# Rearranging the MLP end of an adaLN decode kernel: features on partitions

## The chip, the cores and the metric

The kernel runs on one core of a Trainium2 chip. A core has TensorE (PE: matmuls, with a separate weight load, PEld), VectorE (DVE), ScalarE (ACT), GpSimd (POOL) and SyncE (SP), which here only issues transfers; 16 DMA engines carry them. SBUF is the on-chip memory of 128 partitions, PSUM the memory that matmuls write. The metric is device time in microseconds (us), the median of several runs.

## The reference

One decode step for four sequences (one new token each): adaLN modulation, attention over a cache of 4096 positions in 32 heads, then a gated MLP. The inputs are bfloat16.

```python
x = A_x                                          # (4, 1, 512)
mod = (_silu(c) @ w_mod).reshape(c.shape[0], 6, 1, -1)
sa, ca, ga, sb, cb, gb = (mod[:, i] for i in range(6))
h = _layernorm(x, axis=-1) * (1 + ca) + sa
x = x + ga * _A_ref(h, A_k_cache, A_v_cache, A_wq, A_wo)
h = _layernorm(x, axis=-1) * (1 + cb) + sb
x = x + gb * _B_ref(h, B_w_in, B_w_sp, B_b_sp, B_w_out)

def _B_ref(x, w_in, w_sp, b_sp, w_out):          # w_in 512 x 1792, w_out 896 x 512
    z = _gelu(jnp.einsum('bsd,df->bsf', x, w_in))
    z1 = z[..., :Fh].copy()
    z2 = _layernorm(z[..., Fh:], axis=-1)
    g = jnp.einsum('ts,bsf->btf', w_sp, z2) + b_sp[None, :, None]
    return jnp.einsum('bsf,fd->bsd', z1 * g, w_out)
```

`_A_ref` is ordinary attention: queries from `wq`, scores scaled by 128 ** -0.5, softmax, the sum over V, and the projection by `wo`. The sequence length is 1, so `w_sp` and `b_sp` are one number each. The K and V caches are 128 MB each and make up nearly all of the transfer.

## The kernel before

The order of instructions on each engine is the order of the program; nothing is moved by a scheduler. The attention runs over NT = 32 steps, each one pair of four heads (`HQ`) and one sequence, with a K tile and a V tile of 4 MB. SP issues all large loads in one queue: the modulation and query weights first, then K and V tiles, at step 2 `wo_sb` and `wo_last` (the projection weights of all groups but the last, and of the last), and in the last steps V in pieces (`TAIL`: 64, 32, 16 and 16 of 128 column blocks), then `win_sb` and `wout_sb` (L505, L507). A step multiplies K by the query on VectorE (L278), reduces it on TensorE (L284) and VectorE (L293), takes the softmax, and two steps later V is summed (`pv`, L353).

Step 2 also makes the modulation columns (`mod_cols`, L232: features on partitions, the four sequences as columns) and the gate rows `gps` (L477, copied to `gbr` at L482), which step 5 multiplies by the two numbers `w_sp` and `b_sp`.

The last step L is one of sequence `BL` = 3, the last row. Its V is summed by `o_last` (L389) in four parts that follow the pieces of `TAIL`, with V as the stationary operand. Between the parts, TensorE does the two products of the second layernorm for the rows known so far: `normed` (its `across` at L185 sums over partitions by a matrix of constants, its `summed` at L190 adds the blocks). Rows 0 to 2 are complete there; row 3 still lacks the last group of heads. That contribution, `last` (L540), is scaled and added after `o_scale` (L395) and `o_proj` (L405), and a second product (`st`, `mq2`) gives row 3's own mean and variance.

Then the MLP:

- L552: 56 matmuls, `win_sb` stationary, `hcs` moving. `hcs` has eight columns: the four rows as normed without their scale, and the four shifts `sb`. The scales `rs2` are made on ACT meanwhile (`rsqrt`, L194 and L195: Ln, then Exp) and are applied to the product by VectorE at L574; L575 adds the product of the shifts.
- L562 loads ACT's table for gelu, L577 and L581 take the gelu of the second half (`z2`, the gate) and of the first (`z1`), and L582 loads the table for Ln and Exp again.
- L583 and the `across` after it: sums of `z2` and of its square for the gate's layernorm.
- L593 (`w_out`): two passes of 28 matmuls each, with `z1w` (z1, in 32 columns, the unused ones zero) and `pw` (z1 * z2) as the stationary operand and `wout_sb` moving, 128 columns at a time; the four blocks of 128 output columns go to four column groups of TensorE. The outcome has rows on partitions.
- L604 to L617: the layernorm's mean and variance for each of these partitions, with a second Ln and Exp; L620 to L629: six operations on 128x128 tiles that put the two passes, the gate rows and the residual `x1r` (L568: the residual brought to the same layout by 16 small matmuls) together.
- L633: four transfers write the output.

Of the kernel before, what the change touches and what calls it, by code (L numbers as in the profile page):

```python
# [22 lines left out]
def kernel(  # L23
# [112 lines left out]
    st3 = consts.tile([P, 2, B, NH + 1], F32, name="st3")  # L136
    nc.vector.memset(st3, 0.0)
    nc.vector.memset(st3[:, 1, :, NH:], LN_EPS * FH / P)
# [7 lines left out]
    selb = consts.tile([P, B], F32, name="selb")  # L146
    idr = ident_f.rearrange("p (c g q) -> p g c q", g=R // HQ, q=HQ)
    for g in range(G):
        nc.vector.tensor_reduce(out=selg[:, g:g + 1], in_=idr[:, g], axis=AX.XY, op=ALU.add)
    nc.vector.tensor_reduce(  # L150
        out=selb, in_=ident_f.rearrange("p (c b) -> p b c", b=B), axis=AX.X, op=ALU.add
    )
    nc.vector.tensor_copy(out=sel4, in_=selb)
# [4 lines left out]
    z1w = consts.tile([P, NH, R], BF16, name="z1w")  # L158
    nc.gpsimd.memset(z1w, 0.0)
    pw = consts.tile([P, NH, R], BF16, name="pw")  # L160
    nc.gpsimd.memset(pw, 0.0)
    cTw = consts.tile([P, DJ, R], BF16, name="cTw")
    nc.gpsimd.memset(cTw, 0.0)
# [33 lines left out]
    def normed(pool, src, name, then=None):  # L197
# [11 lines left out]
        nc.vector.tensor_tensor(out=sq, in0=xb, in1=xb, op=ALU.mult)  # L209
        v = summed(pool, across(sq, inv_d), f"v_{name}")  # L210
# [14 lines left out]
    cT = cTw[:, :, 0:B]  # L225
    nc.vector.tensor_tensor(out=cT, in0=cx, in1=sg, op=ALU.mult)

    def mod_cols(s0, n, dst):
        for m in range(n):
            c0 = (s0 + m // DJ) * D + m % DJ  # L230
            for k in range(DJ):
                nc.tensor.matmul(  # L232
                    dst[:, m, :], lhsT=wm_sb[:, k, c0:c0 + (P - 1) * DJ + 1:DJ], rhs=cT[:, k, :],
                    start=(k == 0), stop=(k == DJ - 1),
                )
# [180 lines left out]
    hcs = consts.tile([P, DJ, 2 * B], BF16, name="hcs")  # L416
    gbr = consts.tile([P, P], F32, name="gbr")
    gbw = consts.tile([P, P], F32, name="gbw")
# [14 lines left out]
    for i in range(NT):  # L433
# [33 lines left out]
        if i == 2:  # L467
            nc.scalar.dma_start(out=sp_t[:, 0:1], in_=B_w_sp[0:1, 0:1])
            nc.scalar.dma_start(out=sp_t[:, 1:2], in_=B_b_sp.rearrange("(a b) -> a b", b=1))
            mps = ps_sm([P, 3 * DJ, B])  # L470
            mod_cols(2, 3 * DJ, mps)
            nc.vector.tensor_copy(out=modT, in_=mps)
            nc.vector.tensor_copy(out=hcs[:, :, B:2 * B], in_=mps[:, DJ:2 * DJ, :])
            gps = ps_sm([P, P])
            for k in range(DJ):
                for j in range(DJ):
                    nc.tensor.matmul(  # L477
                        gps[R * j:R * (j + 1), :], lhsT=cTw[:, k, :],
                        rhs=wm_sb[:, k, 5 * D + j * P:5 * D + (j + 1) * P],
                        start=(k == 0), stop=(k == DJ - 1), tile_position=(0, R * j),  # L480
                    )
            nc.vector.tensor_copy(out=gbr, in_=gps)  # L482
# [8 lines left out]
            nc.sync.dma_start(out=wo_last, in_=A_wo[hl:H * DH].rearrange("(q p) n -> p q n", p=P))  # L491
        if i == 5:
            sps = ps_sm([P, 2])
            nc.tensor.matmul(sps, lhsT=ones_b, rhs=sp_t, start=True, stop=True)
            nc.vector.tensor_copy(out=spf, in_=sps)
            for k, t in ((0, gbw), (1, gbr)):
                nc.vector.tensor_scalar(
                    out=t, in0=gbr, scalar1=spf[:, k:k + 1], scalar2=None, op0=ALU.mult
                )
            cbT = modT[:, 2 * DJ:3 * DJ, :]  # L500
            nc.vector.tensor_scalar_add(out=cbT, in0=cbT, scalar1=1.0)
# [7 lines left out]
    gaT = modT[:, 0:DJ, :]  # L509
    scores(L)  # L510
# [20 lines left out]
    xc, rs2 = normed(tl, x1, "ln2", lambda: o_last(L, 1))  # L531
    hc = hcs[:, :, 0:B]
    nc.vector.tensor_tensor(out=hc, in0=xc, in1=cbT, op=ALU.mult)

    o_last(L, 2)
    o_last(L, 3)
    o_scale(L)
# [6 lines left out]
    mq2 = summed(tl, across(st2, inv_d), "mq2")  # L544
    nc.vector.scalar_tensor_tensor(
        out=hc[:, :, BL], in0=xs, scalar=mq2[:, 0:1], in1=cbT[:, :, BL],
        op0=ALU.subtract, op1=ALU.mult,
    )
    zps = ps_q()[:, 0:NF * 2 * B].rearrange("p (f b) -> p f b", b=2 * B)
    for f in range(NF):  # L550
        for k in range(DJ):
            nc.tensor.matmul(  # L552
                zps[:, f, :], lhsT=win_sb[:, k, f * P:(f + 1) * P], rhs=hcs[:, k, :],
                start=(k == 0), stop=(k == DJ - 1),
            )
# [5 lines left out]
    rsqrt(rs2[:, BL:B], nv2, -1.0)  # L561
    nc.scalar.preload_act_table_set("gelu_apprx_tanh_and_others")  # L562
    nc.vector.tensor_tensor(out=x1[:, :, BL], in0=x1[:, :, BL], in1=last, op=ALU.add)
    x1r = ps_red()[:, 0:P]
    for k in range(DJ):
        for j in range(DJ):
# [4 lines left out]
            )  # L571

    z = tl.tile([P, NF, B], F32, name="z")
    nc.vector.tensor_tensor(out=z, in0=zps[:, :, 0:B], in1=bc(rs2, NF), op=ALU.mult)  # L574
    nc.vector.tensor_tensor(out=z, in0=z, in1=zps[:, :, B:2 * B], op=ALU.add)  # L575
    z2 = st3[:, 0, :, 0:NH]
    nc.scalar.activation(  # L577
        out=z2, in_=z[:, NH:, :].rearrange("p f b -> p b f"), func=AF.Gelu_apprx_tanh
    )
    z1 = tl.tile([P, NH, B], F32, name="z1")  # L580
    nc.scalar.activation(out=z1, in_=z[:, 0:NH, :], func=AF.Gelu_apprx_tanh)  # L581
    nc.scalar.preload_act_table_set("natural_log_exp_and_others")  # L582
    nc.vector.tensor_tensor(out=st3[:, 1, :, 0:NH], in0=z2, in1=z2, op=ALU.mult)  # L583
    ps3 = across(st3.rearrange("p g b f -> p g (b f)"), inv_f)
# [79 lines left out]
```

## Time and profile before

| what | us |
|---|---|
| median of 3 runs | 675.5 |
| the runs | 673.76, 675.5, 675.64 |
| the profiled execution, whole | 673.46 |
| its span, first to last instruction | 671.7 |
| TensorE busy | 405.1 (60%) |
| VectorE busy | 423.3 (63%) |
| ACT busy | 85.0 (13%) |
| GpSimd busy | 3.3 (0%), 15 instructions |
| DMA: bytes, mean rate | 283.19 MB, 422 GB/s |
| chain that ended last: DMA, VectorE, TensorE | 53%, 31%, 14% |
| last transfers issued, from SP and ACT | 668.90 |

The page cuts the span into 40 slices; a digit is the busy share in tenths.

```profile
PE   1185784466577655555666566666556457755766
DVE  3176593775666777566577666666776566777733
DMA  9999999999999999999999999999999999999994
```

The DMA engines are full in every slice but the last, which begins near 655 us. Times below are counted from the start of the span. In timeline lines, the columns are start and length in us, engine, source line, operation, what it writes from what, and in brackets how long its engine had been idle and what ended that.

### The profile page before, as it was taken

To read this page: it belongs to the slowest core of one execution; us is meant where nothing else is said; L and a number is where in the kernel's file an instruction comes from. 1 tells how busy PE (TensorE), PEld (TensorE's weight loads), DVE (VectorE), ACT (ScalarE), POOL (GpSimd) and SP (SyncE) were. 2 spreads that over 40 slices of the span, in tenths; PEclk is the share of its full clock that TensorE was granted. 3 is DMA by queue.
4 is the path that set the end of the run, shared out by engine and by line. 5 is a ranking of instruction groups with operands and counts; after the bars stand their busy time and mean duration, and the time that the engine had idled before them with its cause. 6 is when DMAs were issued, how large, how long until landed. Compare 5 with 4: busy or idle time off the path is not lost.

```text
span 671.7 us, 7155 instructions
## 1 busy us (share of the span) xinstructions
PE 405.1 (60%) x2971; PEld 183.0 (27%) x2971; DVE 423.3 (63%) x620; ACT 85.0 (13%) x278; POOL 3.3 (0%) x15
## 2 busy tenths in 40 slices
PE   1185784466577655555666566666556457755766
PEld 1032332222223222222222222223222223322325
DVE  3176593775666777566577666666776566777733
ACT  1012120111011111101111110111111011111112
POOL 1000000000000000000000000000000000000000
PEclk9998988677888777889867777887777898777975
DMA  9999999999999999999999999999999999999994
GB/s 375 437 431 433 422 410 422 434 427 426 434 432 428 433 430 427 434 435 428 426 432 431 435 430 431 425 431 432 432 430 435 426 430 433 433 426 426 436 414 168
DMA packets 13556, 283.19 MB, mean 422 GB/s; under 512 B 1228, under 2 KB 2644, under 8 KB 4692
## 3 DMA queue, kind: packets, MB, share of 16 engines
q1 hardware_dynamic: 13488, 282.73, 98.5%
q8 instruction: 23, 0.38, 0.2%
q14 instruction: 9, 0.07, 0.0%
q10 hardware_dynamic: 36, 0.01, 0.0%
HBM read 282.73 MB, written 0.00 MB: 421 GB/s over the span
## 4 chain that ended last, share of the span: by engine, by line
DMA 53%; DVE 31%; PE 14%; issue 1%; ACT 0%; SPq 0%; DVEq 0%
DMA kt<-in_A_k_cache_dram 53%; DVE kt L278 22%; PE red L284 11%; DVE osb L365 3%; DVE S L293 2%; PE ops L353 1%; DVE osb L361 1%; DVE mrow L302 1%; DVE mt L306 1%; DVE rz L344 1%; PE qps L389 1%; DVE nM L308 0%; DVE mb L304 0%; DVE nM L309 0%; PE sm L185 0%
## 5 line engine op out<-in xcount | busy, mean ns | idle before, releaser
L284 PE MATMUL red<-kt,ident_bf 128*128 128x512 bf16 x1024 | 304.0, 464 | 235.8 <-DVE kt L278 235.8
L278 DVE TENSOR_TENSOR kt<-kt,qbc 128x8192 bf16<-128x8192 bf16 x64 | 282.8, 4420 | 193.6 <-DMA kt<-in_A_k_cache_dram 192.6
L284 PEld LDWEIGHTS <-ident_bf 128*128 128x128 bf16 x1024 | 117.0, 114 | 411.0 <-issue 285.3
L316 ACT ACTIVATE pbd<-S,nM 32x128 bf16<-32x128 f32 x128 | 73.9, 577 | 508.2 <-DVE nM L309 465.2
L353 PE MATMUL ops<-vt,pbd 128*16 128x512 bf16 x992 | 60.3, 386 | 0.0
L293 DVE TENSOR_REDUCE S<-red 128x64 f32<-128x512 f32 x64 | 43.7, 682 | 8.2 <-PE red L284 8.1
L365 DVE SCALAR_TENSOR_TENSOR osb<-ops,selg,osb 128x128 f32<-128x128 f32 x93 | 32.6, 351 | 3.3
L316 ACT ACTIVATION_READ_ACCUMULATOR pbd<-S,nM 32x1 f32 x128 | 32.1, 251 | 0.0
L353 PEld LDWEIGHTS <-pbd 128*16 128x16 bf16 x992 | 22.3, 90 | 23.2 <-issue 1.7
L264 PE MATMUL qps<-wq_sb,hTb 128*32 128x512 bf16 x128 | 9.2, 412 | 9.2 <-DMA wq_sb<-in_A_wq_dram 8.5
L331 PEld LDWEIGHTS sm<-rsb,ones_f 128*128 128x128 f32 x64 | 12.3, 195 | 4.5
L361 DVE TENSOR_SCALAR osb<-ops,selg 128x128 f32<-128x128 f32 x31 | 10.8, 348 | 3.6 <-PE ops L353 2.9
L379 PEld LDWEIGHTS sm<-sel,osb 128*64 128x64 f32 x224 | 9.2, 138 | 11.9 <-issue 11.4
L379 PE MATMUL sm<-sel,osb 128*64 128x2 f32 x224 | 11.6, 205 | 0.0
L268 ACT CAST qbc<-qps 128x512 bf16<-128x512 f32 x8 | 4.7, 585 | 47.8 <-PE qps L264 47.8
L302 DVE TENSOR_REDUCE mrow<-S 128x1 f32<-128x128 f32 x32 | 9.2, 286 | 1.1
L344 DVE RECIPROCAL rz<-sm 64x2 f32<-64x2 f32 x56 | 9.1, 163 | 0.4
L331 PE MATMUL sm<-rsb,ones_f 128*128 128x4 f32 x64 | 9.3, 215 | 0.0
L324 DVE TENSOR_SCALAR rsb<-mask,rs 128x4 f32<-128x4 f32 x32 | 7.2, 224 | 2.4 <-ACT pbd L316 2.4
L306 DVE STREAM_TRANSPOSE mt<-mb 128x32 f32<-128x32 f32 x32 | 6.8, 212 | 1.1
L264 PEld LDWEIGHTS <-hTb 128*32 128x32 bf16 x128 | 3.1, 100 | 13.3 <-issue 10.6
L308 DVE TENSOR_REDUCE nM<-mt 128x1 f32<-128x32 f32 x32 | 6.0, 186 | 1.1
(129 smaller groups left out, 87.6 us busy)
## 6 DMA issues: line engine op xcount, KB each, us to landing
kt<-in_A_k_cache_dram SPq DMA_DIRECT2D x31, 4096.0 KB, 22.9
vt<-in_A_v_cache_dram SPq DMA_DIRECT2D x31, 4096.0 KB, 30.7
wq_sb<-in_A_wq_dram SPq DMA_DIRECT2D x1, 4096.0 KB
kt<-in_A_k_cache_dram SPq DMA_DIRECT2D x2, 2048.0 KB, 20.4
wo_sb<-in_A_wo_dram SPq DMA_DIRECT2D x1, 3584.0 KB
wm_sb<-in_w_mod_dram SPq DMA_DIRECT2D x1, 3072.0 KB
kt<-in_A_v_cache_dram SPq DMA_DIRECT2D x1, 2048.0 KB
win_sb<-in_B_w_in_dram SPq DMA_DIRECT2D x1, 1792.0 KB, 32.7
```

The source lines that it names most:

```text
L278: nc.vector.tensor_tensor(out=kt, in0=kt, in1=bc(qbc[:, g, b, :], KC), op=ALU.mult)
L284: nc.tensor.matmul(red, lhsT=ident_bf, rhs=kt[:, :, m * RD:(m + 1) * RD], start=(m == 0), stop=(m == DH // RD - 1),)
L293: nc.vector.tensor_reduce(out=st[i, "S"][:, kc * KC:(kc + 1) * KC], in_=st.pop((i, "red", kc)), axis=AX.X, op=ALU.add,)
L302: nc.vector.tensor_reduce(out=mrow, in_=S, axis=AX.X, op=ALU.max)
L306: nc.vector.transpose(mt, mb)
L316: nc.scalar.activation(out=pbd[r, :, q], in_=S[r, :], func=AF.Exp, bias=nM[r, :], scale=att_scale, accum_out=rs[r, :],)
L331: nc.tensor.matmul(z, lhsT=ones_f, rhs=st.pop((i, "rsb")), start=True, stop=True)
L344: nc.vector.reciprocal(out=rz[h, 0, :], in_=z[h, a:HQ:2])
L353: nc.tensor.matmul(opss[i % 2][g:g + G * HQ], lhsT=pbds[i % 3][:, n, :], rhs=vts[i][:, n, :], start=(m < 4), stop=(m >= NJ // G - 4), tile ...
L361: nc.vector.tensor_scalar(out=osb, in0=ops[:, 0, :], scalar1=selg[:, 0:1], scalar2=None, op0=ALU.mult)
L365: nc.vector.scalar_tensor_tensor(out=osb, in0=ops[:, g, :], scalar=selg[:, g:g + 1], in1=osb, op0=ALU.mult, op1=ALU.add,)
L379: nc.tensor.matmul(op[64 * a:64 * (a + 1), r, :], lhsT=osb[:, r:P:2], rhs=sel4[:, a:HQ:2], start=True, stop=True, tile_position=(0, 64 * a),)
```

## The change

The modulation's gate `gb` is made as columns instead of rows (`gsT`, `gwT`, `g8`), and everything after the input matmuls keeps features on partitions until the end:

- `wo_last` is loaded in two transfers, of 8 and of 120 partitions.
- The third and fourth part of `o_last` and `o_scale` move from behind the variance product of `normed` to ahead of it (`sums`).
- Rows 0 to 2 of the MLP's input are scaled and shifted on GpSimd, row 3 on VectorE after its scale `rsl`; `hT2` has four columns where `hcs` had eight. The residual's row 3 is added on GpSimd too.
- The residual's 16 small matmuls go ahead of the input matmuls; their result is copied to SBUF, and a PSUM tile `rows` is cleared.
- The input matmuls run as two halves (`gate`), second half first, and gelu reads PSUM itself.
- `zz` holds z1 and z1 * z2 side by side (eight columns, the first by a product with ones), and one pass of 28 matmuls with `wout_sb` as the stationary operand gives `y`.
- Mean, variance and gate scale small tiles (at most 128x32); three products with the identity, each in four column groups, turn the three terms into rows and add them in PSUM. One operation adds the residual.

```diff
@@ setup
-    st3 = consts.tile([P, 2, B, NH + 1], F32, name="st3")
-    nc.vector.memset(st3, 0.0)
-    nc.vector.memset(st3[:, 1, :, NH:], LN_EPS * FH / P)
+    st3 = consts.tile([P, 3, B, NH], F32, name="st3")
+    nc.vector.memset(st3[:, 0], 1.0)
...
-    z1w = consts.tile([P, NH, R], BF16, name="z1w")
-    nc.gpsimd.memset(z1w, 0.0)
-    pw = consts.tile([P, NH, R], BF16, name="pw")
-    nc.gpsimd.memset(pw, 0.0)
-    cTw = consts.tile([P, DJ, R], BF16, name="cTw")
-    nc.gpsimd.memset(cTw, 0.0)
+    cT = consts.tile([P, DJ, B], BF16, name="cT")
@@ def normed(pool, src, name, then=None, last=None):
         nc.vector.tensor_tensor(out=sq, in0=xb, in1=xb, op=ALU.mult)
+        if last:
+            last()
         v = summed(pool, across(sq, inv_d), f"v_{name}")
@@ step 2
-            mps = ps_sm([P, 3 * DJ, B])
+            mps = ps_sm([P, 4 * DJ, B])
             mod_cols(2, 3 * DJ, mps)
-            nc.vector.tensor_copy(out=modT, in_=mps)
-            nc.vector.tensor_copy(out=hcs[:, :, B:2 * B], in_=mps[:, DJ:2 * DJ, :])
-            gps = ps_sm([P, P])
...
-            nc.vector.tensor_copy(out=gbr, in_=gps)
+            mod_cols(5, DJ, mps, 3 * DJ, True)
+            nc.vector.tensor_copy(out=modT, in_=mps[:, 0:3 * DJ, :])
+            nc.vector.tensor_copy(out=gsT, in_=mps[:, 3 * DJ:, :])
...
-            nc.sync.dma_start(out=wo_last, in_=A_wo[hl:H * DH].rearrange("(q p) n -> p q n", p=P))
+            wl = A_wo[hl:H * DH].rearrange("(q p) n -> p q n", p=P)
+            for r in (slice(0, 8), slice(8, P)):
+                nc.sync.dma_start(out=wo_last[r], in_=wl[r])
@@ after the loop
-    xc, rs2 = normed(tl, x1, "ln2", lambda: o_last(L, 1))
-    hc = hcs[:, :, 0:B]
-    nc.vector.tensor_tensor(out=hc, in0=xc, in1=cbT, op=ALU.mult)
-
-    o_last(L, 2)
-    o_last(L, 3)
-    o_scale(L)
+    def sums():
+        o_last(L, 2)
+        o_last(L, 3)
+        o_scale(L)
+
+    xc, rs2 = normed(tl, x1, "ln2", lambda: o_last(L, 1), sums)
     wp = o_proj(NQ - 1, BL, B)
...
-    mq2 = summed(tl, across(st2, inv_d), "mq2")
-    nc.vector.scalar_tensor_tensor(
-        out=hc[:, :, BL], in0=xs, scalar=mq2[:, 0:1], in1=cbT[:, :, BL],
-        op0=ALU.subtract, op1=ALU.mult,
-    )
...
+    ps2 = across(st2, inv_d)
+    nc.gpsimd.tensor_tensor(out=x1[:, :, BL], in0=x1[:, :, BL], in1=last, op=ALU.add)
...
+    nc.gpsimd.tensor_tensor(out=hf, in0=xc, in1=cbT, op=ALU.mult)
+    nc.gpsimd.tensor_tensor(out=hf, in0=hf, in1=bc(rs2, DJ), op=ALU.mult)
+    nc.gpsimd.tensor_tensor(out=hT2[:, :, hr], in0=hf[:, :, hr], in1=sbT[:, :, hr], op=ALU.add)
+    mq2 = summed(tl, ps2, "mq2")
     nv2 = tl.tile([P, 1], F32, name="nv2")
...
-    rsqrt(rs2[:, BL:B], nv2, -1.0)
+    rsl = tl.tile([P, 1], F32, name="rsl")
+    rsqrt(rsl, nv2, -1.0)
     nc.scalar.preload_act_table_set("gelu_apprx_tanh_and_others")
+    hl = tl.tile([P, DJ], F32, name="hl")
+    nc.vector.scalar_tensor_tensor(
+        out=hl, in0=xs, scalar=mq2[:, 0:1], in1=cbT[:, :, BL], op0=ALU.subtract, op1=ALU.mult
+    )
+    nc.vector.scalar_tensor_tensor(
+        out=hT2[:, :, BL], in0=hl, scalar=rsl, in1=sbT[:, :, BL], op0=ALU.mult, op1=ALU.add
+    )
...
+    x1s = tl.tile([P, P], F32, name="x1s")
+    nc.vector.tensor_copy(out=x1s, in_=x1r)
+    rows = ps_sm([P, P])
+    nc.vector.memset(rows, 0.0)
+
+    def gate(h):
+        z = ps_red()[:, 0:NH * B].rearrange("p (f b) -> p f b", b=B)
+        for f in range(NH):
+            for k in range(DJ):
+                n0 = (h * NH + f) * P
+                nc.tensor.matmul(
+                    z[:, f, :], lhsT=win_sb[:, k, n0:n0 + P], rhs=hT2[:, k, :],
+                    start=(k == 0), stop=(k == DJ - 1),
+                )
+        return z.rearrange("p f b -> p b f")
+
+    zp = gate(1)
+    nc.scalar.activation(out=st3[:, 1], in_=zp, func=AF.Gelu_apprx_tanh)
+    nc.vector.tensor_tensor(out=st3[:, 2], in0=st3[:, 1], in1=st3[:, 1], op=ALU.mult)
+    zp = gate(0)
+    z1 = tl.tile([P, B, NH], F32, name="z1")
+    nc.scalar.activation(out=z1, in_=zp, func=AF.Gelu_apprx_tanh)
     nc.scalar.preload_act_table_set("natural_log_exp_and_others")
+    ps3 = across(st3[:, 1:3].rearrange("p g b f -> p (g b f)"), inv_f)
...
+            out=zz[:, :, g, :].rearrange("p f b -> p b f"), in0=z1, in1=st3[:, g], op=ALU.mult
...
+    for j in range(DJ):
+        for f in range(NH):
+            nc.tensor.matmul(
+                y[:, j], lhsT=wout_sb[:, f, j * P:(j + 1) * P], rhs=zz[:, f],
+                start=(f == 0), stop=(f == NH - 1),
+            )
+    mq3 = tl.tile([P, 2, B], F32, name="mq3")
...
+    nc.vector.tensor_tensor(out=rs3, in0=mq3[:, 0], in1=mq3[:, 0], op=ALU.mult)
+    nc.vector.tensor_tensor(out=rs3, in0=mq3[:, 1], in1=rs3, op=ALU.subtract)
+    rsqrt(rs3, rs3, 1.0, eps)
...
+    nc.vector.tensor_tensor(out=vb, in0=y[:, :, 0, :], in1=gsT, op=ALU.mult)
+    nc.vector.tensor_tensor(
+        out=g8, in0=g8, in1=rs3[:, None, None, :].to_broadcast([P, DJ, 2, B]), op=ALU.mult
+    )
+    nc.vector.tensor_tensor(out=g8, in0=g8, in1=y, op=ALU.mult)
+
+    terms = (vb, g8[:, :, 0, :], g8[:, :, 1, :])
+    for n, t in enumerate(terms):
+        for j in range(DJ):
+            nc.tensor.matmul(
+                rows[R * j:R * j + B, :], lhsT=t[:, j, :], rhs=ident_f,
+                start=(n == 0), stop=(n == len(terms) - 1), tile_position=(0, R * j),
+            )
     xo = tl.tile([P, P], BF16, name="xo")
-    nc.vector.tensor_tensor(out=xo, in0=w, in1=u, op=ALU.add)
+    nc.vector.tensor_tensor(out=xo, in0=rows, in1=x1s, op=ALU.add)
```

## The prediction

> **What bounds the kernel now.** I read the chain of waits first, to see where the transfers stop setting the end. The last K tile lands at 623.46 us; from there the chain is compute alone, 48 us long (two lines of it; columns: start, length, what):
>
> ```profile
> 605.35 18.11 DMA kt<-in_A_k_cache_dram
> 623.48 4.43 DVE kt L278
> ...
> 668.59 0.29 DVE xo L629
> ```
>
> Everything ahead of 623 us is stream time, which this change leaves at the same bytes. The last V pieces and both MLP weights stream beside the 48 us, so I asked next when they land, by two-microsecond windows (last two columns: busy share of the 16 DMA engines, GB/s) and by the issues (us from issue to landing):
>
> ```profile
> 659.00:661.00 2.00, 1.40 (x44) 1.26 (x41) 0.64 (x5) 0.50 (x2) 0.00 (x0) 0.50 0.78 299
> 661.00:663.00 2.00, 1.16 (x23) 1.08 (x24) 0.81 (x6) 0.38 (x2) 0.00 (x0) 0.50 0.53 176
> 663.00:665.00 2.00, 1.67 (x73) 1.51 (x70) 0.46 (x3) 1.63 (x4) 0.00 (x0) 0.50 0.28 91
> ```
>
> ```profile
> win_sb<-in_B_w_in_dram SPq DMA_DIRECT2D x1, 1792.0 KB, 32.7
> wout_sb<-in_B_w_out_dram SPq DMA_DIRECT2D x1, 896.0 KB, 34.8
> ```
>
> win_sb was issued at 629.7, so it lands at 662.4; wout_sb, issued at 630.1, at 664.9. These two are floors under any faster tail. The engines end unevenly: half of them work on after 661. TensorE's granted clock is 0.50 here, so matmul prices must come from this stretch. The timeline of it:
>
> ```profile
> 658.74 0.99 PE L389 MATMUL qps<-pbd,kt 128*128 128x4 bf16 x32
> 659.99 0.67 PE L405 MATMUL sm<-oTs,wo_last 128*128 128x1 bf16 x16 [0.25 <-DVE oTs L395]
> 661.94 0.17 DVE L190 TENSOR_REDUCE mq<-sm 128x2 f32<-128x10 f32 x1 [0.69 <-PE sm L185]
> 662.29 0.21 DVE L557 SCALAR_TENSOR_TENSOR nv<-mq 128x1 f32<-128x1 f32 x1
> 662.44 1.65 PE L552 MATMUL qps<-hcs,win_sb 128*128 128x8 bf16 x56 [0.53 <-DVE hcs L545]
> 662.59 0.20 ACT L194 ACTIVATE rs_ln<-nv 128x1 f32<-128x1 f32 x1 [2.91 <-DVE x1w L563]
> 662.83 0.20 ACT L195 ACTIVATE rs_ln<-rs_ln 128x1 f32<-128x1 f32 x1
> 663.05 1.28 ACT L562 ACT_TABLE_LOAD   x1
> 664.85 0.21 ACT L581 ACTIVATE z<-z 128x28 f32<-128x28 f32 x1
> 665.08 1.28 ACT L582 ACT_TABLE_LOAD   x1
> 665.83 0.94 PE L593 MATMUL red<-wout_sb,z1w 128*32 128x128 bf16 x28
> 666.56 0.96 PE L593 MATMUL sm<-wout_sb,pw 128*32 128x128 bf16 x28
> 668.59 0.29 DVE L629 TENSOR_TENSOR xo<-w,u 128x128 bf16<-128x128 f32 x1
> ```
>
> The reader is to see three things: the input matmuls (L552) start without waiting for the last row's scale, which ACT makes beside them; two passes over w_out end at 667.52; and the page-wide epilogue of VectorE follows until 668.88.
>
> **Part by part**, on the clock of this trace.
>
> *Sums of the last V pieces ahead of the variance (step 1).* The 64 matmuls of parts 2 and 3 now follow part 1 directly. One costs 26.4 ns: (0.99 - 0.17) / 31, 0.17 being one matmul's own time. The second half of part 1 started at 657.44, so 64 of them end at 657.44 + 63 x 0.0264 + 0.17 = 659.27, where 659.73 was. The variance product (0.45 us of PE issue, 658.30 to 658.74) goes behind them and covers o_scale's 0.26 us between the last sum and o_proj: o_proj starts at 659.6 (was 659.99). Gain 0.39. It leans on V having landed: win_sb is behind V in the queue and takes 1,792 KB / 422 GB/s = 4.3 us, so V is in by about 658.1; part 3 starts at 658.7.
>
> *Last row scaled ahead of the matmul (step 2).* `last`, xs, squares, product and mq2 keep their spacing: mq2 at 661.55, the variance nv2 at 661.76 to 661.97. Before, TensorE started 0.50 us after mq2's start. Now it waits for nv2, Ln, Exp and one more VectorE operation: Ln 0.09 after nv2 as now (662.06), Exp 0.24 later (662.30 to 662.50), the last row of hT2 662.53 to 662.77 (0.24, as L545), first input matmul 662.82. That is 0.38 later than 662.44: this part costs 0.77 and eats step 1. The floor of 662.4 is passed by 0.4.
>
> *The other three rows on GpSimd.* Four operations new to the tail, in its order: the last row of x1, then three for hT2. They start after `last` ends (660.46) and must end by about 662.75: 2.25 us, 0.56 each. Nothing stands behind them on GpSimd but the end, but TensorE's 32 transposes of x1 (0.65 us, now ahead of the input matmuls in its order) wait for the first. No row shows a GpSimd operation on two tensors; nearest (timeline of the start):
>
> ```profile
> 1.24 0.20 POOL masks.py:197 MEMSET ident_f<- 128x128 f32 x1
> 1.51 0.29 POOL masks.py:199 TENSOR_SCALAR_AFFINE_SELECT ident_f<-ident_f 128x128 f32<-128x128 f32 x1
> ```
>
> The second waited for the first and started 0.07 after it. Below: 0.10 (its 128x1 memset) + 0.07; above: 0.49 (its 128x512 memset, 1.46 / 3) + 0.07 = 0.56, exactly the room. I take 0.29 + 0.07: 1.4 us in all, done at 661.9, hidden by the chain of step 2 with 0.8 to spare. Without that cover it would cost its whole length. The x1 transposes then run from 661.4 to 662.1, in TensorE's wait; VectorE copies their result (0.3, as L620) and clears `rows` from 662.8 to 663.3, idle until the square at 664.1.
>
> The Trainium skill (GPSIMD Engine Reference, Instruction dispatch) speaks against this part: a first call to freshly loaded GpSimd code pays about 6 us beside a software dispatch. No row here shows such a wait, in front of the select either. By that rule the first matmul would start near 668 and the time be some 5 us longer; by the rows, nothing.
>
> *Gate half first, gelu from PSUM (step 3).* 56 matmuls as before, at (1.65 - 0.17) / 55 = 27 ns. The first 28 end at 662.82 + 0.90 = 663.72. The gelu table starts to load after Exp, 662.52, and is in at 663.80, so the first gelu runs 663.82 to 664.07, its square until 664.29; the second half ends at 664.47, its gelu runs 664.51 to 664.72. The two scaling operations L574, L575 (0.5 us) are gone. z1's gelu was 664.85: the tail is now 0.34 ahead.
>
> *One pass over w_out (step 4).* Two zz operations, started 0.11 apart as z1w and pw were (0.18 and 0.20): 664.75 to 665.06. The product for the sums sits ahead on TensorE, 664.35 to 665.0. 28 matmuls from 665.10, wout_sb in by 0.2: 0.90, end 666.00. Before, 667.52.
>
> *Scales and rows (step 5).* mq3 665.08, two small operations to 665.70; the log table, started 0.23 after the gelu as now, is in at 666.02. Ln 666.04 (0.30, from L194's 128x4), Exp 666.37 to 666.58, two operations on g8 of 0.21 and 0.04 to hand over: 667.05. The term with vb runs in the meantime. Left on the path: 8 products of f32, 128 columns each, 16 rows of PE. No row has this shape. The f32 product of L185 takes 0.60 with 16 columns and 0.69 with 64, so 0.94 ns a column and pass. All 8 in a line with two passes: 8 x 2 x 128 x 0.94 ns + 0.17 = 2.1 us; four column groups at once, as L593's 28 in 0.94 us (23 ns each with 128 columns) show for bf16: 0.65. I take 0.75, nearer to L593, which has the same placing. The page-wide u and w operations give way to xo alone: start 667.05 + 0.04 + 0.75 + 0.04 = 667.89, was 668.59. **Sum: -0.70 us.** Bounds by the f32 products alone: -0.80 to +0.65.
>
> *Far ahead of the tail.* Sixteen more small products and fewer copies near 79 us, memsets gone: TensorE and VectorE wait for K there, nothing. SP issues wo_last in two pieces. Before:
>
> ```profile
> 80.26 19.62 SPq L491 DMA_DIRECT2D wo_last<-in_A_wo_dram  x1
> ```
>
> The K load behind it went out at 100.04. One more issue costs 0.33 to 0.51 of SP (its loads' issues); the queues hold work through it (DMA share 0.92 to 1.05 from 95 to 107 us), so 0, at most 0.5. What the split does to the spread of 512 KB over the engines no row shows: at most 512 KB / 422 GB/s = 1.2 us either way; I take 0.
>
> The skill (DMA: Bandwidth & Descriptors, Why a DMA increments its semaphore by 16) says a copy uses the largest number of engines up to 16 that divides its outer count: 8 rows go to 8 engines, 120 to 15. By it one engine is spared 32 KB, about 1.2 us at a sixteenth of 422 GB/s, and eight get 0.16 us more; a gain only if that one alone is last. Half the engines are late together above, so by the trace about nothing.
>
> Span 671.7 - 0.7 = 671.0; the profiled execution's own 673.46 becomes 672.8. Its time lies 2.0 under the median, 675.5, so the forecast is 675.5 - 0.7 = **674.8**.
>
> **Rivals.**
> 1. *As summed* (0.58): 674.8, alone within 673.4 to 676.0 (-0.3 to -1.2 and half the runs' spread of 1.88).
> 2. *f32 products in a line* (0.10): 1.35 more, 676.15. For it: no row of f32 with column groups of 128 columns. Against: L593.
> 3. *GpSimd becomes the wait* (0.15), slower: it decides from 0.56 us an operation, undoes the gain at 0.74, and at 1.0 ends at 660.5 + 4 x 1.07 = 664.8, two later than 662.77: 676.8. Beyond 0.3% it needs 1.25 each. For: four in a row on an engine idle since 4 us. Against: all its rows are under 0.5.
> 4. *The stream ends it* (0.07): win_sb and wout_sb 0.7 later than here, the gain is gone: 675.5.
> 5. *The split evens the stream* (0.10): 1.2 off every landing and the sum on top: 673.6.
>
> 0.3% of 675.5 is 2.0 us, about what these runs can tell from no change. Below 673.5: most of case 5 and the low edge of case 1 by the runs' spread, 0.18. Above 677.5: the upper part of cases 3 and 2, 0.10. Range 672.6 to 676.9.
>
> **What would show it.** o_proj of the last row near 659.6; the first input matmul near 662.8 with VectorE as releaser, not GpSimd or a DMA; GpSimd's four under 0.5 us each; w_out's pass as 28 matmuls ending near 666.0; 24 f32 rows, of which the last 16 take under 0.9 us; xo near 667.9. A GpSimd operation above 0.74 us, last products above 1.5 us, or K's landing off 623.5 by more than 1 us would make it wrong.

## The result and the profile after

The changed kernel takes 676.54 us (median of 17 runs, 675.86 to 677.47), the kernel before 674.43 (17 runs, 673.67 to 675.64). The ratio is 1.0029, with a 95% interval of 1.0022 to 1.0036: some 2 us slower, where 0.7 us faster was forecast. The difference lies just within the 0.3% that three runs can tell; seventeen runs tell it from no change. The time is inside the range, but the sign is wrong, and that it is inside is luck: the range reached up to 676.9 for slow GpSimd operations and slow f32 products, and neither is what made it slower.

Three questions are to be asked of the profile: does the tail do what was summed, when does it start, and what comes behind it? The chain of waits of the changed kernel answers the second (start, length, what):

```profile
607.53 17.98 DMA kt<-in_A_k_cache_dram
625.54 4.42 DVE kt L275
...
631.42 33.77 DMA win_sb<-in_B_w_in_dram
665.24 1.67 PE red L581 x56
...
670.57 0.29 DVE xo L636
```

The last K tile's multiplication starts at 625.54; before, it was 623.48. The stream is 2.06 us late with the same bytes. And win_sb's landing, not the compute, now releases the input matmuls (by little, as the timeline will show). Lines of the timeline of the changed kernel's tail, to be held against the one of before (start, length, engine, line, operation):

```profile
661.88 0.66 PE L402 MATMUL sm<-oTs,wo_last 128*128 128x1 bf16 x16
663.46 0.22 POOL L545 TENSOR_TENSOR hf<-hf,rs_ln 128x16 f32<-128x16 f32 x1
663.75 0.21 POOL L546 TENSOR_TENSOR hT<-hf,modT 128x12 bf16<-128x12 f32 x1
664.76 0.23 DVE L560 SCALAR_TENSOR_TENSOR hT<-hl,rsl,modT 128x4 bf16<-128x4 f32 x1 [0.37 <-ACT rsl L188]
665.24 1.65 PE L581 MATMUL red<-hT,win_sb 128*128 128x4 bf16 x56 [0.86 <-DMA win_sb<-in_B_w_in_dram]
667.71 0.91 PE L604 MATMUL qps<-zz,wout_sb 128*128 128x8 bf16 x28 [0.29 <-DVE mq L609]
669.47 1.03 PE L631 MATMUL sm<-ident_f,g 128*4 128x128 f32 x16
670.57 0.29 DVE L636 TENSOR_TENSOR xo<-sm,x1s 128x128 bf16<-128x128 f32 x1 [1.16 <-PE sm L631]
670.89 0.65 SPq L640 DMA_DIRECT2D out_dram<-xo  x2
670.89 0.86 ACTq L640 DMA_DIRECT2D out_dram<-xo  x2
```

The compute of the tail is shorter: from the first input matmul to the start of xo it takes 670.57 - 665.24 = 5.33 us, where 668.59 - 662.44 = 6.15 was. GpSimd is no wait. But it all comes 2 us later, and behind xo something is new: ACT's two output issues take 0.86 us together, and from xo's end (670.86) to the end of the span (674.8) it is 3.9 us; before it was 671.7 - 668.88 = 2.8, with this issue:

```profile
668.91 0.62 ACTq L633 DMA_DIRECT2D out_dram<-xo  x2
```

For the bookkeeping I cut both profiled spans at three points: the start of the 64 matmuls of the first part of `o_last` ("sums over V"; before, then after), the start of xo, the end of the span.

```profile
655.30 1.85 PE L389 MATMUL qps<-pbd,kt 128*128 128x4 bf16 x64
657.61 1.85 PE L386 MATMUL qps<-pbd,kt 128*128 128x4 bf16 x64
```

| stretch | before | after | difference |
|---|---|---|---|
| start to the sums over V | 655.30 | 657.61 | +2.3 |
| sums over V to xo | 13.29 | 12.96 | -0.3 |
| xo and what follows | 3.1 | 4.2 | +1.1 |
| span | 671.7 | 674.8 | +3.1 |

These two profiled executions lie 3.1 us apart, the medians 2.1. Of the first row's 2.3 us, 2.06 are the last K tile's; the rest comes between it and the sums, a stretch that took 30.8 us in one run below and 32.2 in another, and is not followed up here. The experiments ask where the first and the third row come from, and what the second would be alone.

### The profile page after: what moved, and what is told of

Same layout as the page of the kernel before. It is cut to its first block, busy times and chain, and to the rows that moved or that the text cites. A ratio compares the mean times of both kernels' runs of the same rounds, so it can differ in the third digit from the quotient of the medians.

```text
span 674.8 us, 7140 instructions
## 1 busy us (share of the span) xinstructions
PE 399.3 (59%) x2967; PEld 181.7 (27%) x2967; DVE 420.7 (62%) x614; ACT 85.1 (13%) x278; POOL 3.5 (1%) x16
## 4 chain that ended last, share of the span: by engine, by line
DMA 58%; DVE 28%; PE 12%; issue 1%; SPq 0%; ACT 0%; DVEq 0%
DMA kt<-in_A_k_cache_dram 53%; DVE kt L275 21%; PE red L281 10%; DMA win_sb<-in_B_w_in_dram 5%; DVE osb L362 2%; DVE S L290 1%; DVE osb L358 1%; DVE mrow L299 1%; DVE rz L341 1%; PE ops L350 1%; DVE mt L303 0%; DVE nM L305 0%; DVE mb L301 0%; DVE nM L306 0%; PE sm L229 0%
## 5 line engine op out<-in xcount | busy, mean ns | idle before, releaser
L281 PE MATMUL red<-kt,ident_bf 128*128 128x512 bf16 x1024 | 296.9, 456 | 243.6 <-DVE kt L275 243.6
L281 PEld LDWEIGHTS <-ident_bf 128*128 128x128 bf16 x1024 | 115.3, 113 | 413.3 <-issue 278.4
```

What stands on the lines that cost most here:

```text
L281: nc.tensor.matmul(red, lhsT=ident_bf, rhs=kt[:, :, m * RD:(m + 1) * RD], start=(m == 0), stop=(m == DH // RD - 1),)
```

## The experiments

Ratios are against the kernel before, measured beside each run on the same chip, with 95% intervals. Medians of different experiments can come from different chips, so the ratios are the safer comparison.

### Where the stream loses two microseconds

The only edit ahead of the tail that touches transfers is the split of wo_last. First it is taken out of the changed kernel (*e1_after_whole*):

```diff
-            wl = A_wo[hl:H * DH].rearrange("(q p) n -> p q n", p=P)
-            for r in (slice(0, 8), slice(8, P)):
-                nc.sync.dma_start(out=wo_last[r], in_=wl[r])
+            nc.sync.dma_start(out=wo_last, in_=A_wo[hl:H * DH].rearrange("(q p) n -> p q n", p=P))
```

> The changed kernel with wo_last loaded in one transfer again; the rest of the change stays. Theory 'uneven split': the 2.0 us by which the last K tile landed late (625.5 against 623.5) come back, and the tail keeps its gain: K lands near 623.5, the first input matmul starts at 662.4 to 662.9, and the time is 0.4 to 1.0 us under the kernel before, ratio 0.9985 to 0.9995. Rival 'more work at step 2' (sixteen more matmuls, wo_sb issued 0.4 us later): K still lands near 625.5 and the ratio stays near 1.003.

Then it is put into the kernel before, alone: 8 and 120 partitions (*e2_before_8_120*), 64 and 64 (*e3_before_64_64*), 16 and 112 (*e4_before_16_112*), and last two transfers of two heads each, which both cover all 128 partitions (*e5_before_heads*):

```diff
-            nc.sync.dma_start(out=wo_last, in_=A_wo[hl:H * DH].rearrange("(q p) n -> p q n", p=P))
+            wl = A_wo[hl:H * DH].rearrange("(q p) n -> p q n", p=P)
+            for r in (slice(0, 8), slice(8, P)):          # e2; e3: 64, e4: 16
+                nc.sync.dma_start(out=wo_last[r], in_=wl[r])
+            for r in (slice(0, 2), slice(2, HQ)):         # e5, in place of the loop above
+                nc.sync.dma_start(out=wo_last[:, r, :], in_=wl[:, r, :])
```

> The kernel before with nothing changed but wo_last loaded in two transfers, of 8 and of 120 partitions. Theory 'uneven split': the stream loses about 2 us between 95 and 115 us, packets of 1 KB take near 81 ns instead of 48, K lands near 625.5, and the time is 2.0 to 2.8 us over the kernel before (ratio 1.0030 to 1.0042). Rival 'more work at step 2': no change, ratio 0.9995 to 1.0005.

> The kernel before with wo_last in two transfers of 64 partitions each, which both divide evenly over 16 engines. Theory 'uneven split': no loss, ratio within 0.9993 to 1.0007. Rival 'one more transfer' (the loss is from a second transfer in SP's queue, whatever its shape): about 2 us more, ratio near 1.003.

> The kernel before with wo_last in two transfers of 16 and 112 partitions: both divide over 16 engines (1 and 7 partitions each), but an engine's partitions are no longer the ones it has in a load of 128. Theory 'fewer engines' (the loss is from 120 rows on 15 engines): no loss, ratio within 0.9993 to 1.0007. Rival 'shifted partitions' (the loss is from engines writing partitions that others write too): packets of 1 KB near 80 ns and a loss of 1 us or more, ratio over 1.0015.

> The kernel before with wo_last in two transfers again, this time cut by heads: each has all 128 partitions and two heads. Theory 'shifted partitions' (an engine that serves other partitions than in a load of 128 gets in the way of engines still at the load before): packets of 1 KB stay near 48 ns and nothing is lost, ratio within 0.9990 to 1.0010. Rival 'one more transfer': packets near 80 ns or not, the loss of 1.5 to 2.6 us seen with the cuts by partitions comes back, ratio 1.0020 or more.

| kernel | median | ratio [95%] | last K multiplied from |
|---|---|---|---|
| e1: changed, wo_last whole | 674.58 | 1.0005 [0.9995, 1.0016] | 623.89 |
| e2: before, 8 and 120 | 676.39 | 1.0032 [1.0020, 1.0045] | 625.64 |
| e3: before, 64 and 64 | 677.40 | 1.0039 [1.0024, 1.0053] | 626.98 |
| e4: before, 16 and 112 | 675.92 | 1.0023 [1.0013, 1.0034] | 626.22 |
| e5: before, by heads | 674.56 | 1.0012 [1.0001, 1.0023] | 623.60 |

One window shows the place. wo_last is issued near 80 us and flows behind the tiles queued ahead of it: its 512 packets of 1 KB go out from 106.5 to 109.9 us in the kernel before, and from 106.7 to 112.8 in the changed one. The rows below are that window in six kernels, in this order: before, changed, e2, e3, e4, e5 (stretch, its length, busy time and count of PE, PEld, DVE, ACT, POOL, the granted clock; the last two columns are the DMA share and GB/s):

```profile
106.00:112.00 6.00, 6.00 (x41) 2.67 (x43) 0.19 (x1) 0.00 (x0) 0.00 (x0) 0.74 1.11 427
```

```profile
106.00:112.00 6.00, 6.00 (x34) 2.59 (x36) 0.62 (x2) 0.00 (x0) 0.00 (x0) 0.72 1.16 315
```

```profile
106.00:112.00 6.00, 6.00 (x41) 2.59 (x43) 0.30 (x1) 0.00 (x0) 0.00 (x0) 0.72 1.23 327
```

```profile
106.00:112.00 6.00, 5.56 (x50) 2.55 (x49) 0.89 (x4) 0.00 (x0) 0.00 (x0) 1.00 1.21 296
```

```profile
106.00:112.00 6.00, 6.00 (x38) 2.54 (x40) 0.52 (x1) 0.00 (x0) 0.00 (x0) 0.72 1.24 298
```

```profile
106.00:112.00 6.00, 6.00 (x34) 2.54 (x36) 0.65 (x2) 0.00 (x0) 0.00 (x0) 0.72 1.10 423
```

The share shows that the engines are no less busy (1.16 to 1.24 against 1.11), but they move a quarter to a third less: 315, 327, 296 and 298 GB/s where the transfer is cut by partitions, 427 and 423 where it is not. (427 - 315) GB/s x 6 us = 0.67 MB, or 1.6 us of stream at 420 GB/s. In the packet records the 1 KB packets of wo_last show it too: a median of 48 ns each in the kernel before and in e5, 81 in the changed kernel and in e2, 86 in e3, 89 in e4. And so do the neighbours: the 32 KB packets of the K and V tiles that start in this window take 1.22 us in the median before and 1.21 in e5, but 1.75 in the changed kernel and 1.84 to 2.26 in e2 to e4. Nothing later wins it back, since the DMA engines are full until the end.

So the loss is that of the cut. e1 and e2 show it from both sides: -2.0 us where the split is taken out of the change (676.54 to 674.58; 1.6 by the ratios), +1.9 where it alone is put in (674.45 to 676.39; 2.2 by the ratio). Of the reasons I had, three fell. That one more issue on SP costs it: e5 has it too, with the stream in its place, and is 0.1 to 1.6 us slower by its interval (0.4 by the medians, 674.56 against 674.16 beside it), which may be the issue; its packets show nothing of the loss. That the pieces are uneven: e3 is even, and the slowest by its median. That 8 and 120 rows go to fewer than 16 engines, the rule that the prediction weighed (the Trainium skill, DMA: Bandwidth & Descriptors, Why a DMA increments its semaphore by 16): 64 and 64, and 16 and 112, all divide by 16 and lose 2.6 and 1.6 us by the ratios. What is left is that the transfer no longer covers all partitions. The same page (The descriptor swizzle) says that in a transfer to 128 partitions each engine writes a fixed set of partitions of its own; a cut by partitions would then have engines write where others are writing for the tiles around it. That fits all five runs, but none shows which engine wrote which partition: an inference. The cut also changes which rows of DRAM are read side by side, and no run separates the two.

### What the tail gains

Step 1 alone on the kernel before (*e6_before_sums*); and 16 more modulation matmuls at step 2, whose result nothing uses (*e7_before_more*), for the prediction's zero there:

```diff
+    def sums():
+        o_last(L, 2)
+        o_last(L, 3)
+        o_scale(L)
+
-    xc, rs2 = normed(tl, x1, "ln2", lambda: o_last(L, 1))
+    xc, rs2 = normed(tl, x1, "ln2", lambda: o_last(L, 1), sums)
...
-    o_last(L, 2)
-    o_last(L, 3)
-    o_scale(L)
@@ e7, step 2
-            mps = ps_sm([P, 3 * DJ, B])
-            mod_cols(2, 3 * DJ, mps)
+            mps = ps_sm([P, 4 * DJ, B])
+            mod_cols(2, 4 * DJ, mps)
...
```

> The kernel before with step 1 of the change alone: the third and fourth part of the V sums ahead of the variance product. Theory 'the weights' landing is the floor': o_proj starts about 0.35 us earlier, counted from the second part of the sums, but the first input matmul waits for win_sb, which lands where it did; ratio 0.9992 to 1.0008 and TensorE's wait ahead of the input matmuls is put down to the DMA of win_sb. Rival 'compute sets the tail': the whole 0.4 us shows at the end, ratio about 0.9994, and the input matmuls follow VectorE's last hcs as before.

> The kernel before with the sixteen modulation matmuls of the change added at step 2 (their result is not used; the gate rows are made as before). wo_sb is issued 0.4 to 0.6 us later. Theory 'the queue holds work': nothing lost, ratio 0.9992 to 1.0008. Rival 'step 2 delays the stream' (which would be where the gain of the rearranged tail went): 0.4 to 0.8 us more, ratio 1.0006 to 1.0012, and K lands that much later.

e7: 674.45, 1.0003 [0.9994, 1.0013]: nothing, as taken. e6: 674.34, 1.0004 [0.9994, 1.0015]; a gain of up to 0.4 us lies inside this interval, so the time alone can't say that the earlier sums bring nothing. Its timeline says where they went:

```profile
662.65 0.24 DVE L548 SCALAR_TENSOR_TENSOR hcs<-st,mq,modT 128x4 bf16<-128x4 f32 x1
664.84 1.66 PE L555 MATMUL qps<-hcs,win_sb 128*128 128x8 bf16 x56 [2.43 <-DMA win_sb<-in_B_w_in_dram]
```

The input is ready at 662.89, and the matmuls wait 1.95 us longer, for win_sb. This profiled execution had a late stream (last K from 625.17; 675.96 us, the slowest of its runs), so the size of the wait is not typical. The floor itself is: in the kernel before, win_sb lands at 662.4, just as the matmuls that use it start (662.44), and in e2 to e5 and e7 its landing ends TensorE's wait there too. The same shows in e1, the changed kernel with wo_last whole:

```profile
662.19 0.23 DVE L558 SCALAR_TENSOR_TENSOR hT<-hl,rsl,modT 128x4 bf16<-128x4 f32 x1 [0.37 <-ACT rsl L188]
662.91 1.66 PE L579 MATMUL red<-hT,win_sb 128*128 128x4 bf16 x56 [1.10 <-DMA win_sb<-in_B_w_in_dram]
...
668.24 0.29 DVE L634 TENSOR_TENSOR xo<-sm,x1s 128x128 bf16<-128x128 f32 x1 [1.16 <-PE sm L629]
...
668.57 0.86 ACTq L638 DMA_DIRECT2D out_dram<-xo  x2
```

hT is ready at 662.42, 0.49 us before win_sb lets the matmuls go; where nothing else is awaited the way from hT to the first matmul is 0.14 (e10, below). So 0.35 us of what was won ahead of this point is lost to the stream. From the matmuls on it is 5.33 us to xo, as in the changed kernel.

The last products were the step with the widest bounds. *e8_after_one_product* (wo_last whole) adds the three terms on VectorE first, in another order of additions, and makes the rows by one product in place of three:

```diff
-    vb = tl.tile([P, DJ, B], F32, name="vb")
-    nc.vector.tensor_tensor(out=vb, in0=y[:, :, 0, :], in1=gsT, op=ALU.mult)
+    g3 = tl.tile([P, DJ, 3, B], F32, name="g3")
+    nc.vector.tensor_tensor(out=g3[:, :, 2, :], in0=y[:, :, 0, :], in1=gsT, op=ALU.mult)
...
-    nc.vector.tensor_tensor(out=g8, in0=g8, in1=y, op=ALU.mult)
+    nc.vector.tensor_tensor(out=g3[:, :, 0:2, :], in0=g8, in1=y, op=ALU.mult)
+    g1 = tl.tile([P, DJ, B], F32, name="g1")
+    nc.vector.tensor_reduce(
+        out=g1, in_=g3.rearrange("p j g b -> p j b g"), axis=AX.X, op=ALU.add
+    )
-    terms = (vb, g8[:, :, 0, :], g8[:, :, 1, :])
+    terms = (g1,)
```

> The changed kernel with wo_last whole, and the three terms added on VectorE (one reduction) before one product with the identity instead of three. Theory 'f32 products cost 64 ns a row of PE': the last product takes 0.6 us where two took 1.03, the reduction costs 0.25, and the stretch from win_sb's landing to xo shortens by 0.15 to 0.25 us. Rival 'the latency of a product dominates, not its rows': the product still takes 0.9 us or more and the stretch grows. In the time, ratio 0.998 to 1.001 to the kernel before in either case.

674.41, 1.0008 [0.9999, 1.0017]. Its timeline:

```profile
668.50 0.21 DVE L626 TENSOR_REDUCE g<-g 128x16 f32<-128x48 f32 x1
668.85 0.61 PE L633 MATMUL sm<-ident_f,g 128*4 128x128 f32 x8 [1.30 <-DVE g L626]
```

8 rows of f32 take 0.61 us, 16 took 1.03: (1.03 - 0.61) / 8 = 53 ns a row in four column groups. For bf16 it is 27: in the kernel before, groups of four L593 matmuls start 107 ns apart. The sum costs 0.21 and the way to and from it, so from the first input matmul to xo's end it is 5.50 us where e1 takes 5.62. That is 0.1 us, a little under the 0.15 to 0.25 expected, and the medians don't tell the two kernels apart.

### What comes behind the output

e1 has the stream in its place and a shorter tail, and is still no faster than before. From xo's end to the end of its span it takes 672.2 - 668.53 = 3.7 us, against 2.8 before. The transfers between 668 and 673 us, in 40 slices of 0.125 us, of the kernel before and of e1 (GB/s of each slice):

```profile
GB/s 66 0 0 0 0 0 0 0 0 0 0 0 0 17 0 0 10 6 0 0 0 0 0 0 0 0 0 0 0 0 0 0 0 0 0 0 0 0 0 0
```

```profile
GB/s 0 0 0 0 0 0 0 0 0 0 10 6 0 6 66 6 0 0 4 0 0 0 0 0 0 0 0 0 0 0 0 0 0 0 0 0 0 0 0 0
```

The slice of 66 is one packet of 8 KB on queue 14, which the page of transfers calls an instruction fetch; the small numbers are the output. Before, the fetch is past before the output is issued. In e1 it stands between the output's packets. SP's wait for the output at the end of the program (total us, count, longest), before and in e1:

```profile
SPq L659 <- DMA out_dram<-xo: 1.0, 1, 1.0
```

```profile
SPq L664 <- DMA out_dram<-xo: 1.8, 1, 1.8
```

The theory: the fetch belongs to an engine's instructions, and comes when that engine reaches a certain count of them. The change leaves ACT with 198 instructions instead of 199 and VectorE with 7 or 8 fewer, so the fetch comes at another moment. (This is the count in the program, waits and issues included; ACT's missing one is a wait. The page's count of 278 for ACT leaves those out and is the same in both kernels.) Against it: SP's count, GpSimd's four operations, or the output's own form. Each run below but e13 starts from e1:

```diff
@@ e9, after the memset of eps: VectorE
+    idle = consts.tile([P, 8], F32, name="idle")
+    for k in range(8):
+        nc.vector.memset(idle[:, k:k + 1], 0.0)
@@ e10, the same place: ACT
+        nc.scalar.copy(out=idle[:, k:k + 1], in_=eps)
@@ e11: the last row of x1 and the three operations of hT2
-    nc.gpsimd.tensor_tensor(...)
+    nc.vector.tensor_tensor(...)
@@ e12, step 2
-            nc.scalar.dma_start(out=sp_t[:, 0:1], in_=B_w_sp[0:1, 0:1])
-            nc.scalar.dma_start(out=sp_t[:, 1:2], in_=B_b_sp.rearrange("(a b) -> a b", b=1))
+            nc.sync.dma_start(out=sp_t[:, 0:1], in_=B_w_sp[0:1, 0:1])
+            nc.sync.dma_start(out=sp_t[:, 1:2], in_=B_b_sp.rearrange("(a b) -> a b", b=1))
@@ e13, the kernel before: only the second of these two lines
```

> The changed kernel with wo_last whole and eight more tiny VectorE memsets near the start. In the runs so far the stretch from the end of xo to the end of the span is 2.8 us in kernels with the old tail and 3.4 to 3.9 us in kernels with the new one, where 8 KB of instructions (queue q14) come between the output's packets instead of ahead of xo. Theory 'VectorE's instruction fetch': eight more instructions ahead bring its boundary forward, the 8 KB move ahead of xo, the stretch is 2.8 us again and the time 0.6 to 0.9 us less than with wo_last whole alone, ratio 0.9985 to 0.9998 to the kernel before. Rival 'another engine's': nothing moves, 3.5 us, ratio 1.000 to 1.001.

> The changed kernel with wo_last whole and eight tiny ACT copies near the start. Theory 'ACT's instruction fetch' (ACT issues its second output transfer 0.27 us later in the new tail): the 8 KB move ahead of the output, the stretch from xo's end to the span's end is 2.8 us and the time falls by 0.6 to 0.9 us, ratio 0.9985 to 0.9998. Rival 'another engine's': 3.5 us as before, ratio 1.000 to 1.001.

> The changed kernel with wo_last whole and the four GpSimd operations of the tail on VectorE instead. Theory 'GpSimd sets the late fetch' (its only instructions since 4 us): the stretch from xo's end to the span's end is 2.8 us. Rival 'not GpSimd': 3.5 us. In the tail VectorE has four operations of about 0.2 us more between the squares of the last row and mq2, of which the product across partitions (0.6 us) covers most, so the first input matmul starts 0 to 0.4 us later; ratio 0.999 to 1.001.

> The changed kernel with wo_last whole and the two 2-byte loads of w_sp and b_sp issued by SP instead of ACT, so that SP has three instructions more (158, the kernel before has 156, with wo_last whole it is 155) and ACT two fewer. Theory 'SP's instruction fetch': its boundary comes earlier, ahead of the wait for xo, the 8 KB move ahead of the output, the stretch from xo's end is 2.8 us and the time falls by 0.6 to 0.9 us, ratio 0.9985 to 0.9998. Rival 'another engine's': 3.5 us, ratio 1.000 to 1.001.

> The kernel before with one of its two 2-byte loads issued by SP instead of ACT: ACT has 198 instructions, as the changed kernel has, where the kernel before has 199. Nothing else changes. Theory 'ACT's count places the fetch': the 8 KB of instructions come between the output's packets, the stretch from xo's end to the span's end grows from 2.8 to about 3.6 us, ratio 1.0008 to 1.0015. Rival 'the new tail itself makes the end longer': 2.8 us as before, ratio 0.9993 to 1.0007.

| kernel | ACT's instructions | median | ratio [95%] | xo's end to the end |
|---|---|---|---|---|
| before | 199 | 674.43 | 1 | 2.8 |
| e1 | 198 | 674.58 | 1.0005 [0.9995, 1.0016] | 3.7 |
| e9: VectorE +8 | 198 | 674.40 | 1.0003 [0.9994, 1.0011] | 3.8 |
| e10: ACT +8 | 206 | 673.03 | 0.9982 [0.9973, 0.9991] | 2.7 |
| e11: no GpSimd | 198 | 674.23 | 1.0001 [0.9992, 1.0011] | 3.5 |
| e12: two loads from ACT to SP | 196 | 673.59 | 0.9988 [0.9979, 0.9997] | 2.8 |
| e13: before, one load to SP | 198 | 674.82 | 1.0006 [0.9996, 1.0016] | 3.6 |

The end is long wherever ACT has 198 instructions, and short with 196, 199 and 206; VectorE's count and GpSimd do nothing to it. Nor does SP's: the kernel before and the changed one have 156 SP instructions each, e12 and e13 158 each, and in both pairs one end is short and one long. Queue 14 carries such packets for other engines too: in e9 VectorE's eight instructions brought one forward from 634.1 (e1) to 621.2 us, and left the last where it was, 1.6 us behind xo's start. In e10, eight idle copies at the start of the program bring the last fetch forward to 648.4 us, 20 us ahead of xo, and ACT's output issue is back at its old price (timeline, then the same 5 us of transfers):

```profile
663.16 1.63 PE L582 MATMUL red<-hT,win_sb 128*128 128x4 bf16 x56 [0.76 <-DVE hT L561]
668.48 0.29 DVE L637 TENSOR_TENSOR xo<-sm,x1s 128x128 bf16<-128x128 f32 x1 [1.16 <-PE sm L632]
...
668.80 0.62 ACTq L641 DMA_DIRECT2D out_dram<-xo  x2
```

```profile
GB/s 0 0 0 0 0 0 0 0 0 0 0 0 12 4 0 8 8 0 0 0 0 0 0 0 0 0 0 0 0 0 0 0 0 0 0 0 0 0 0 0
```

In e12 two instructions fewer put the fetch behind the output, where it delays nothing:

```profile
GB/s 0 0 0 0 0 0 0 0 0 0 15 2 0 17 0 0 0 0 0 66 0 0 0 0 0 0 0 0 0 0 0 0 0 0 0 0 0 0 0 0
```

e12 was run for another theory, SP's count, by which the fetch would come earlier. Its time and its end came as that theory said, but the fetch moved the other way: the time alone would have confirmed a wrong cause.

And e13 makes the same long end in the kernel before by taking one instruction from ACT (ACT's issues and SP's wait at its end):

```profile
670.96 0.86 ACTq L633 DMA_DIRECT2D out_dram<-xo  x2
SPq L659 <- DMA out_dram<-xo: 1.7, 1, 1.7
```

Its trace does what was expected; its time, +0.5 us in the median, has an interval that holds 1. So the place of the fetch and what it does to the output's issue and packets are shown; its price in the median lies between the 0.5 us of e13 and the 1.5 of e10 against e1 (674.58 - 673.03), and the profiled ends of e1, e9, e11 and e13 say 0.7 to 1.0.

### Both together

*e14_change_act8* is the changed kernel as it is, split included, with the eight idle copies of e10. *e15_one_product_act8* is e8 with them.

> The changed kernel as it is, wo_last in 8 and 120 partitions, with eight tiny ACT copies near the start. If the parts add up (tail -1.3 us with the fetch out of the way, split +2.0 us), the ratio is 1.0005 to 1.0020, about 1.3 us under the changed kernel, and K and win_sb still land 2 us late. Rival 'the late stream hides it' (with the stream late, the end is set elsewhere): ratio near 1.003.

> wo_last whole, eight tiny ACT copies near the start, and the three terms added on VectorE ahead of one product: the version that should beat both kernels. From the runs so far: 0.1 us under the same kernel with three products, ratio 0.9972 to 0.9992 to the kernel before. Rival: the one product only moved time, ratio as with three or above, 0.998 to 0.9995, which these runs cannot tell apart by the median; the stretch from the first input matmul to xo's end tells: 5.5 us against 5.6.

e14: 676.08 (674.33 to 677.64), 1.0026 [1.0013, 1.0040], above the 1.0005 to 1.0020 expected. The end is short again, 674.8 - 672.02 = 2.8 us, but its profiled execution lost more to the split than the changed kernel's: 289 GB/s between 106 and 112 us, and the last K from 627.54. That the parts add up is thus not shown by its time; the split's loss is not the same in each execution. e15: 673.90, 0.9989 [0.9979, 0.9999], with 5.52 us from the first input matmul to xo's end and 2.8 behind it. No gain over e10 shows. The fastest version is e10: the change with wo_last in one transfer and the fetch out of the way, 673.03 us against 674.28 for the kernel before beside it, 1.2 less (0.6 to 1.8 by the interval).

## Why the prediction was wrong

**The step that failed** is the one far ahead of the tail: "What the split does to the spread of 512 KB over the engines no row shows: at most 512 KB / 422 GB/s = 1.2 us either way; I take 0." It costs about 2 us (e1, e2; 1.3 at the least by e2's interval), more than the bound. The bound itself was wrong in kind: it took the transfer's own time at full rate as the most that could be lost, as if only the spread of bytes over engines could change. The packets got slower, from 48 to 81 ns, and so did those of the neighbours, from 1.22 to 1.75 us (changed kernel). The argument from the page's rule, that half the engines are late anyway, had no row behind it either: a mean busy share of 0.53 does not say how many engines it is. The prediction named the sign that would make it wrong, K's landing off 623.5 by more than 1 us, and it came: 625.54. None of the rivals had it with this sign; rival 5 had the split evening the stream. Rival 4 had the nearest outcome, the weights' landing as the end of the wait, and that came in e1 and the changed kernel, but it gave no reason for a late stream. What was set aside for one more issue, 0 to 0.5, fits e5.

**What was left out:** the sum ended at xo and took everything behind it as before. It is 0.9 to 1.1 us longer (e1, the changed kernel), since ACT has one instruction less (e10, e12, e13). No row of the profile priced that; the fetch was there to be seen in the trace of before, 0.9 us ahead of the output's issue, but nothing in it says what moves it.

**The tail itself** did what the steps said, by the traces of e1 and e10, where the stream is in its place:

- Step 1, -0.39: from the start of the first part of `o_last` to o_proj it was 659.99 - 655.30 = 4.69 us, and is 4.26 in e10 (655.64 to 659.90): -0.43. (The 64 matmuls of the prediction are the 32 of part 1 and the 32 of parts 2 and 3; it has their names wrong, not their number.)
- Step 2, "costs 0.77": from o_proj to the input matmuls 2.45 us before, and 3.26 in e10, where VectorE releases them: +0.81. "The floor of 662.4 is passed by 0.4" held in e10, not in e1 and not in the changed kernel, where win_sb came last, by 0.35 and 0.1 us.
- GpSimd: 0.21 to 0.24 us each, all four in 0.98 us where 1.4 was taken, and done 0.8 us before VectorE's row 3: hidden. Rival 3 fell. The first of them began with its input, after 657 to 660 us of idleness, so the rule of 6 us for a first call (the Trainium skill, GPSIMD Engine Reference, Instruction dispatch) didn't bear on these operations.
- Steps 3 to 5: from the input matmuls to xo 5.33 us, against 6.15 before; 667.89 - 662.82 = 5.07 was forecast. Of the 0.26 missing, the last 16 rows are the most: "I take 0.75", and they took 1.03. The f32 price behind the upper bound applies in part: 53 ns a row, where the prediction had 23 for column groups at the bf16 price (27 by the starts above) and 120 one after the other (0.94 ns x 128). Rival 2 did not come: it needed 2.1.

Without waits the tail gains 0.43 - 0.81 + 0.82 = 0.44 us, where 0.70 was summed. So the change has a small gain that was foreseen, a loss of 2 us in a line that looked like housekeeping, and a loss of about 1 us at a place that it does not touch. With both losses out of the way, the median of e10 says 1.2 us where the trace of its tail says 0.44; where the rest comes from no run shows.

**Open:** why a cut by partitions slows the packets (the runs show that it does, not which engines or partitions meet), why e14 lost more to it than the changed kernel, and why e10 gains more than its tail.

## What to carry to other kernels

Where the DMA engines are full for the whole run, an edit to the shape of a transfer is worth more care than the arithmetic at the end: cut a load so that each part still covers all partitions, and measure the cut alone. When a shorter tail doesn't shorten the time, cut the span at the last operation and look behind it, at the output's issues and at what else moves on the DMA engines there. A tail whose matmuls wait for a weight's landing gains nothing from work moved ahead of that wait.

## What the runs showed of the hardware

- Cutting one 512 KB load by partitions, in a full queue, made its 1 KB packets take 81 to 89 ns instead of 48, the 32 KB packets beside them 1.75 to 2.26 us instead of 1.22, and dropped the rate over 6 us from 427 GB/s to between 296 and 327 (changed kernel, e2 to e4); cutting the same load with all 128 partitions in both parts left it at 48 ns and 423 GB/s (e5).
- One ACT instruction fewer moved an 8 KB instruction fetch from 0.9 us ahead of the output's issue to behind it (e13). Between the output's packets it made ACT's two output issues take 0.86 us instead of 0.62 and SP's wait for the output 1.7 to 2.0 us instead of 1.0 to 1.1.
- Eight instructions that compute nothing made a kernel faster: 674.58 to 673.03 us, ratios 1.0005 and 0.9982 (e1, e10).
